# A Fourier transform along the model dimension: from a product of weight and table to a transform of the values, with its own pipeline

## The chip, the cores and the metric

The kernel runs on one core of one Trainium2 chip. The metric is the device time of one execution in microseconds; before the change it is 658.19 us, the median of 3 runs (657.83 to 658.28). Engines are called PE (TensorE; its weight load PEld), DVE (VectorE), ACT (ScalarE), POOL (GpSimd) and SP (SyncE, which only issues transfers here).

## What is computed

```python
bucket = pack(q @ proj > 0), pack(k @ proj > 0)
attn   = softmax(where(bucket_q == bucket_k, q @ k.T / 8, -1e9)) @ v
x      = attn as (2, 768, 512)
gate   = sigmoid(causal 5-tap convolution of x along s with conv_w)
x2     = (gate * (x @ w_val)) @ w_out
u      = x2 + Re(FFT_d(FFT_s(x2)))
un     = (u - mean(u)) / sqrt(var(u) + 1e-6)
out    = u + relu(un @ w_ch1) @ w_ch2
```

There are 2 batches, 768 positions s, 512 channels d, and 2048 hidden units. Weights arrive as 64-bit floats. The kernel works in a 32-bit format of PE with short mantissas; each factor is kept as a high and a low part, and each product is made of three: high x high, high x low, low x high.

## The kernel before

The work goes through three phases, and on each engine the instructions stand in the order in which the program issues them (nothing is reordered by a scheduler).

`attention()` runs over 96 blocks and ends with the products with w_val of batch 0 (tiles `early` and `late`, L199). In its last two turns DVE also computes the convolution of channel chunk 2 of batch 1 (`conv_dve`, L219 to L226), and POOL splits x into high and low parts (`x_split`, L186 to L189).

`mixing()` has the rest of the first MoE block and the two Fourier transforms. Of the transform along d only 258 columns are computed (NL; 257 cosines or sines and one of padding), the other 255 mirror them; that along s is folded: `even_odd` (L925 to L937) makes the sum and the difference of position s and 768 - s of the gated values. DVE makes them in `gt` (L935 for 383 columns, L936 for one), ACT the high part `gh` (L929), POOL the low part `gl` (L930). With s = 0 (sum) and s = 1 (difference) there are two parts per batch, each of 4 chunks of channels (c) and 3 blocks of 128 folded positions (kt). In order:

- w_out is converted to high and low parts chunk by chunk (`from64`, L125 to L157: DVE L139, ACT L142, DVE L145, L146, L149, L150, L157, ACT L162), with the temporaries `cv` in SBUF. Between the chunks stand the products with w_val of batch 1 (`val`) and the gates (L207). POOL computes the convolution of chunk 3 (L215, L217) and the splits `xsl` (L189).
- PE transposes w_out (L974, 32 of them) and multiplies it with the table of cosines and sines: L984, 8 groups of 12 matmuls of 258 columns. ACT and DVE split the results into `wah` and `wal` (L989, L990).
- For each batch: 7 groups of 12 matmuls of 258 columns give the folded values times that product (L1003 in `gmm`, split into `ah` and `al`, L1016 and L1017); then, for each kt, `own` (12 matmuls of 512 columns with w_out for each s; L1003 too), `mixed` (the transform along s of ah and al, L1049, with a copy by ACT, L1051), `total` (DVE adds both, L1056, L1058, L1061), and POOL makes two blocks of u from sum and difference (L1073). For batch 0 `center` follows (DVE L866 to L868: mean, variance, subtraction), and its transposes (L880, with L883 and L884) stand between the groups of batch 1.
- In batch 1, `channel_split(kt)` for kt = 0 and 1 converts the first weights of the MLP (the same steps L139 to L150, and POOL L155) after the sums of kt and ahead of its u additions.

`channel()` is the MLP: `first` (L1109), relu and split (L1111, L1112), `second` (L1121).

The lines that differ on the way to a single product with the table are the two following; everything else is in the functions below.

```python
pa[:, :NL], w[:, c, m * P : (m + 1) * P], wide[:, x, c, part * NL : (part + 1) * NL],
gmm(pa[:, :NL], b, s, m, lambda c: wah[:, c, part, :], lambda c: wal[:, c, part, :])
```

Of the kernel before, what the change touches and what calls it, by code (L numbers as in the profile page):

```python
# [17 lines left out]
P = 128  # L18
# [30 lines left out]
def dft_tables():  # L49

    d = np.arange(DM)
    l = np.arange(NL)
    ang = 2.0 * np.pi * ((d[:, None] * l[None, :]) % DM) / DM
    cs = 2.0 * np.concatenate([np.cos(ang), np.sin(ang)], axis=1)
    ch, cl = split12(cs)
    wide = np.stack([ch, cl], 0).reshape(2, NC, P, 2 * NL).transpose(2, 0, 1, 3)
# [43 lines left out]
def block_kernel(  # L100
# [118 lines left out]
    def conv_dve(c, i):  # L219

        x, dst = xT[1], g[1][:, c, :]
        if i == 0:
            nc.vector.tensor_scalar_mul(dst, x[:, c, 0:S], cwt[:, 0, c : c + 1])
        for kk in (1, 2) if i == 0 else (3, 4):
            nc.vector.scalar_tensor_tensor(
                dst, x[:, c, kk : kk + S], cwt[:, kk, c : c + 1], dst, op0=ALU.mult, op1=ALU.add  # L226
            )


    def attention(es):  # L230
# [488 lines left out]
        for n in range(NT + 2):  # L719
# [82 lines left out]
            if n >= NT:  # L802
                conv_dve(2, n - NT)
# [7 lines left out]
        for c in range(NC):  # L811
            x_split(1, 0, c, nc.vector)
        for c in range(NC):
# [72 lines left out]
    def mixing(es):  # L886
        mp = pool(es, "mp")
        ps = pool(es, "psx", 8, psum=True)

        def psum():  # L890
            return ps.tile([P, 512], F32, tag="ps", name="ps")
# [3 lines left out]
        wah = mp.tile([P, NC, 2, NL], F32R, name="wah")  # L895
        wal = mp.tile([P, NC, 2, NL], F32R, name="wal")


        ep = pool(es, "ep", 2)
        seq = ep.tile([P, 2, 2, 3, HS], F32R, name="seq", bufs=1)  # L900
        odd = ep.tile([P, 2, P], F32R, name="odd", bufs=1)
        vs = ExitStack()
        vp = pool(vs, "vp", side="right")
        conv_tmp = xT[0].rearrange("p c t -> p (c t)")[:, :S]
        gts = [ep.tile([P, HS], F32, name=f"gt{i}", bufs=1) for i in range(4)]
        rs = ExitStack()
        rp = pool(rs, "rp")
        raws = [rp.tile([P, DM], I64, name=f"wor{c}") for c in range(NC)]
        for c in range(NC):
            nc.sync.dma_start(raws[c], w_out[c * P : (c + 1) * P, :])  # L910
        toh = vp.tile([P, NC, DM], F32R, name="toh")
        tol = vp.tile([P, NC, DM], F32R, name="tol")
        wide = vp.tile([P, 2, NC, 2 * NL], F32R, name="wide")
        xsplit[1, 1] = tuple(vp.tile([P, NC, HS], F32R, name=f"xs{i}") for i in "hl")


        gh, gl = {}, {}

        def parts_tiles(b, pl):
            for s in range(2):  # L920
                gh[b, s] = pl.tile([P, NC, HS], F32R, tag=f"gh{s}", name="gh", bufs=1)
                gl[b, s] = pl.tile([P, NC, HS], F32R, tag=f"gl{s}", name="gl", bufs=1)

# [15 lines left out]
        wo = [from64(rp, raws[c], woh[:, c, :], wol[:, c, :], half=True) for c in range(NC)]  # L939
# [6 lines left out]
        nc.gpsimd.dma_start(wide, t_wide)  # L946
        for i in range(6):
            conv_pool(1, 3, i, conv_tmp)
        for c in range(NC):
            x_split(1, 1, c)  # L950
        for c in range(3):
            sigmoid(1, c)
        for i in range(6, 9):
            conv_pool(1, 3, i, conv_tmp)
        nc.gpsimd.dma_start(seq, t_seq)
        nc.gpsimd.dma_start(odd, t_odd)
        for c in range(NC):
            val(0, c)
        for c in range(NC):
            run(wo[c])  # L960
            val(1, c)
            if c == 3:
                sigmoid(1, 3)
                nc.scalar.activation(warm, warm, AF.Sqrt)
            gate(1, 0, c, pvs[0, c])
        for c in range(NC):
            gate(1, 1, c, pvs[1, c])


        for c in range(NC):  # L970
            for i, (w, to) in enumerate(((woh, toh), (wol, tol))):
                pw = psum()
                for m in range(NC):
                    nc.tensor.transpose(pw[:, m * P : (m + 1) * P], f32(w)[:, m, c * P : (c + 1) * P], ident)  # L974
                nc.scalar.copy(to[:, c, :], pw)
        rs.close()
        pp = pool(es, "pp")
        parts_tiles(0, pp)
        for i, (m, part) in enumerate((m, part) for part in range(2) for m in range(NC)):
            pa = psum()  # L980
            n = 0
            for w, x in ((toh, 0), (toh, 1), (tol, 0)):
                for c in range(NC):
                    nc.tensor.matmul(  # L984
                        pa[:, :NL], w[:, c, m * P : (m + 1) * P], wide[:, x, c, part * NL : (part + 1) * NL],
                        start=n == 0, stop=n == 3 * NC - 1,
                    )
                    n += 1
            nc.scalar.copy(wah[:, m, part, :], pa[:, :NL])  # L989
            nc.vector.tensor_tensor(wal[:, m, part, :], pa[:, :NL], f32(wah)[:, m, part, :], op=ALU.subtract)  # L990
# [4 lines left out]
        vs.close()  # L995
        xs.close()
        m2 = pool(es, "m2", 2)

        def gmm(dst, b, s, m, wh, wl):
            n = 0  # L1000
            for x, w in ((gh[b, s], wh), (gh[b, s], wl), (gl[b, s], wh)):
                for c in range(NC):
                    nc.tensor.matmul(  # L1003
                        dst, x[:, c, m * P : (m + 1) * P], w(c), start=n == 0, stop=n == 3 * NC - 1
                    )
                    n += 1

        parts_tiles(1, m2)
        for b in range(B):
            ah = m2.tile([P, 2, 4, NL], F32R, tag="ah", name="ah", bufs=1)  # L1010
            al = m2.tile([P, 2, 4, NL], F32R, tag="al", name="al", bufs=1)
            todo = [(0, m, 0, m) for m in range(3)] + [(1, 0, 0, 3)] + [(1, m, 1, m) for m in range(3)]
            for i, (s, m, part, slot) in enumerate(todo):
                pa = psum()
                gmm(pa[:, :NL], b, s, m, lambda c: wah[:, c, part, :], lambda c: wal[:, c, part, :])
                nc.scalar.copy(ah[:, part, slot, :], pa[:, :NL])  # L1016
                nc.vector.tensor_tensor(al[:, part, slot, :], pa[:, :NL], f32(ah)[:, part, slot, :], op=ALU.subtract)  # L1017
                if b == 0:
                    even_odd((1, i // 4, i % 4))
                    if i == 6:  # L1020
                        even_odd((1, 1, 3))
                        even_odd()
                        gs.close()
                        late_tiles()
                        channel_load(0)
                        channel_load(1)
                elif i < 6:
                    u_transpose(0, i, psum)
            for kt in range(3):
# [172 lines left out]
```

## Time and profile before

| | |
|---|---|
| median of 3 runs | 658.19 us (657.83 to 658.28) |
| profiled execution | 658.59 us, span 656.8 us |
| granted PE clock, mean | 0.995 |
| PE busy | 636.2 us (97%) |
| DVE busy | 454.3 us (69%) |
| ACT busy | 357.6 us (54%) |
| POOL busy | 275.2 us (42%) |

The span reaches from the first to the last instruction; the execution's own time has 1.8 us more around it. Times in the views count from the start of the span. A row of a timeline gives the start of a group of equal instructions, how long the group lasted, the engine, line, operation, output <- inputs and the count; in brackets how long the engine waited before it and for which instruction. A row of the chain gives start, length and what it was, for the chain of work that ended last. The granted clock is a share of 2.4 GHz.

### The profile page before, as it was taken

The numbers are of one execution on the slowest core, as the hardware profiler recorded it, in microseconds if no ns is written. First come the engines' busy times: TensorE is split into PE (matmuls) and PEld (weight loads), VectorE is DVE, ScalarE is ACT, GpSimd is POOL, SyncE is SP. The second block draws the span as 40 slices with busy tenths as digits, with TensorE's granted clock in tenths as the row PEclk, the third lists the DMA queues.
The fourth block names the chain that finished last, engine by engine and source line by source line (L and its number), as shares of the span: only waits on it lengthen the run. The fifth ranks groups of instructions, "written<-read, shape, count | busy, mean of one in ns | idle before, by whom it ended". The sixth has DMA issues, their size and how long they took to land.

```text
span 656.8 us, 10829 instructions
## 1 busy us (share of the span) xinstructions
PE 636.2 (97%) x3954; PEld 597.1 (91%) x3954; DVE 454.3 (69%) x832; ACT 357.6 (54%) x707; POOL 275.2 (42%) x285
## 2 busy tenths in 40 slices
PE   7999999999999999969999989999999999999997
PEld 6899999999999999869989878999999899999996
DVE  4998999999898987987756478899886511111113
ACT  5888989888798996355313345555665211111110
POOL 7132578788788698925531343333332000000000
PEclk9999999999999999979999999999999999999999
DMA  6957465675755303450000123444441100000002
GB/s 157 202 124 169 128 160 126 145 181 132 188 130 132 92 17 114 153 216 1 1 1 1 54 76 129 128 129 129 128 130 64 70 26 1 0 1 1 0 1 96
DMA packets 54061, 61.32 MB, mean 93 GB/s; under 512 B 28936, under 2 KB 42332, under 8 KB 53752
## 3 DMA queue, kind: packets, MB, share of 16 engines
q1 hardware_dynamic: 53272, 56.02, 32.1%
q0 software_dynamic: 432, 4.60, 1.9%
q8 instruction: 31, 0.51, 0.3%
q14 instruction: 22, 0.18, 0.1%
q10 hardware_dynamic: 304, 0.01, 0.0%
HBM read 35.04 MB, written 3.15 MB: 58 GB/s over the span
## 4 chain that ended last, share of the span: by engine, by line
PE 80%; DVE 11%; POOL 3%; issue 2%; ACT 1%; SPq 1%; DMA 1%; DVEq 0%; POOLq 0%; ACTq 0%
PE pf L1109 19%; PE acc L1121 19%; PE sp L469 8%; PE ps L1003 8%; PE op L529 8%; PE ptp L506 7%; PE ps L1049 2%; PE bp L346 2%; DVE ptl L518 1%; DVE sd L481 1%; PE ptp L601 1%; DVE cv L149 1%; DVE cv L146 1%; PE ps L974 1%; POOL g L217 1%
## 5 line engine op out<-in xcount | busy, mean ns | idle before, releaser
L1121 PE MATMUL acc<-w,hid 128*128 128x512 f32 x576 | 137.1, 390 | 0.0
L1121 PEld LDWEIGHTS acc<-w,hid 128*128 128x128 f32 x576 | 107.4, 188 | 19.8
L1112 DVE SCALAR_TENSOR_TENSOR hid<-pf,hid 128x384 fp32r<-128x384 f32 x60 | 32.2, 555 | 120.0 <-ACT hid L1111 120.0
L481 DVE TENSOR_SCALAR_CACHE_REDUCE sd<-sp 128x768 f32<-128x768 f32 x96 | 91.0, 948 | 16.1 <-PE sp L469 15.2
L518 DVE TENSOR_TENSOR ptl<-ptp,pth 128x768 fp32r<-128x768 f32 x96 | 91.4, 952 | 5.9 <-ACT pth L514 5.9
L1109 PE MATMUL pf<-uth,w 128*128 128x384 f32 x480 | 94.7, 338 | 0.2 <-POOL w L155 0.2
L514 ACT CAST pth<-ptp 128x768 fp32r<-128x768 f32 x96 | 77.3, 805 | 31.0 <-PE ptp L506 13.6
L469 PE MATMUL sp<-k,q 128*128 128x384 f32 x384 | 90.8, 358 | 3.0 <-DVE sd L481 1.7
L488 ACT ACTIVATE sd<-sd,nm 128x768 f32<-128x768 f32 x96 | 90.7, 944 | 2.7 <-DVE sd L481 2.7
L1111 ACT ACTIVATE hid<-pf 128x384 fp32r<-128x384 f32 x60 | 28.0, 488 | 113.9 <-PE pf L1109 113.9
L1109 PEld LDWEIGHTS pf<-uth,w 128*128 128x128 f32 x480 | 85.6, 187 | 3.0 <-POOL w L155 0.5
L155 POOL TENSOR_TENSOR w<-cv 128x512 fp32r<-128x512 f32 x32 | 41.4, 1293 | 107.9 <-DVE cv L150 95.5
L506 PE MATMUL ptp<-ident,sd 128*128 128x128 f32 x576 | 78.6, 273 | 0.2 <-ACT sd L488 0.2
L529 PE MATMUL op<-ptl,v 128*128 128x256 f32 x288 | 73.8, 285 | 0.0
L529 PE MATMUL op<-pth,v 128*128 128x256 f32 x288 | 73.8, 283 | 0.0
L469 PEld LDWEIGHTS sp<-k,q 128*128 128x128 f32 x384 | 62.3, 189 | 6.3 <-DVE sd L481 4.1
L506 PEld LDWEIGHTS ptp<-ident,sd 128*128 128x128 f32 x576 | 65.8, 141 | 1.0 <-ACT sd L488 0.5
L547 POOL TENSOR_TENSOR xm<-xc,xs 64x256 f32<-64x256 f32 x48 | 36.1, 751 | 67.8 <-ACT sd L488 31.6
L142 ACT ACTIVATE cv<-cv,col 128x512 int32<-128x512 int32 (+1 forms) x37 | 26.5, 716 | 57.6 <-DVE cv L139 57.6
L529 PEld LDWEIGHTS op<-ptl,v 128*128 128x128 f32 x288 | 54.7, 190 | 0.9 <-issue 0.2
L529 PEld LDWEIGHTS op<-pth,v 128*128 128x128 f32 x288 | 54.6, 190 | 0.0
L1109 PE MATMUL pf<-utl,w 128*128 128x384 f32 x240 | 52.1, 338 | 0.0
(222 smaller groups left out, 1118.2 us busy)
## 6 DMA issues: line engine op xcount, KB each, us to landing
raw<-in_moe_w_ch_dram SPq DMA_DIRECT2D x32, 512.0 KB, 3.7
q<-ht SPq DMA_DIRECT2D x30, 192.0 KB
k<-ht SPq DMA_DIRECT2D x30, 192.0 KB, 3.1
rqk<-in_q_dram SPq DMA_DIRECT2D x16, 192.0 KB, 3.6
rqk<-in_k_dram SPq DMA_DIRECT2D x16, 192.0 KB, 4.5
rv<-in_v_dram SPq DMA_DIRECT2D x8, 384.0 KB, 3.3
out_dram<-o SPq DMA_DIRECT2D x12, 256.0 KB, 2.1
xs<-xc SPq DMA_DIRECT2D x47, 64.0 KB, 1.9
```

What stands on the lines that cost most here:

```text
L155: nc.gpsimd.tensor_tensor(dst_l, fold(g.bitcast(F32)), fold(e.bitcast(F32)), op=ALU.mult)
L469: nc.tensor.matmul(sp[:, a, :HS], q2[i][:, m, qi * P : (qi + 1) * P], k2[i][:, m, a * HS : (a + 1) * HS], start=m == 1, stop=m == 0,)
L481: nc.vector.tensor_scalar(sd[n].rearrange("p (a c) -> p a c", a=2), sp[:, :, :HS], CLAMP, None, op0=ALU.min, op1=ALU.min, accum_out=st[p][ ...
L488: nc.scalar.activation(sd[n], sd[n], AF.Exp, bias=st[p]["nm"][:, i : i + 1], scale=-1.0, accum_out=st[p]["sums"][:, i : i + 1],)
L506: nc.tensor.transpose(tp[:, r // 3, c0 : c0 + P], sd[n][:, r * P : (r + 1) * P], ident)
L514: nc.scalar.copy(p_parts(n)[0], tp)
L518: nc.vector.tensor_tensor(lo, tp, f32(ho), op=ALU.subtract)
L529: nc.tensor.matmul(po[kb], v3[:, r, c0 : c0 + P], pt[kb][x][:, r, :], start=r == 0 and x == 0, stop=r == R - 1 and x == 1,)
L547: add[kb] = lambda: nc.gpsimd.tensor_tensor(st[p]["xm"][mr, blk * QB : (blk + 1) * QB], xc[mr, :], xs[mr, :], op=ALU.add)
L1003: nc.tensor.matmul(dst, x[:, c, m * P : (m + 1) * P], w(c), start=n == 0, stop=n == 3 * NC - 1)
L1109: nc.tensor.matmul(pf[:, :HS], w[:, c, :], x[:, c, cs], start=n == 0, stop=n == 3 * NC - 1)
L1121: nc.tensor.matmul(acc, x[:, ts_], w, start=f == 0 and n == 0, stop=f == NF - 1 and n == 2)
```

## The change

The two-step product (w_out times table, then values times that) is replaced: the values times w_out (`own`), which were computed anyway, are now also the input of the transform along d.

- `fold`: ACT copies the own product to `y` (L1013); DVE adds or subtracts columns d and 512 - d (L1016), which gives 256 columns in place of 512.
- `turn`: PE transposes these (2 blocks of 128, and for the cosine part a third with the column d = 0; L1024, L1026); ACT and DVE split them into high and low parts `ft` (L1031, L1032).
- `along_d`: PE multiplies them with the table `tab` (6 matmuls of 258 columns, and 2 more with `first` for d = 0 in the cosine part; L1043), ACT and DVE split the result into `ah` and `al` (L1046, L1047).
- `mixed` and `total` stay in what they compute; `total` adds from PSUM into `y` (L1069 to L1074), and the u additions are at L1084, all in `both(b, kt)`.
- The pipeline runs over 12 jobs (b, kt, s): turn i issues `own` and `fold` of job i, `along_d` of job i - 2, `turn` of job i - 1. The three `both(0, kt)` all stand in turn 7; the transposes of u of batch 0 in turns 11 to 13; the three `both(1, kt)` behind the pipeline, the first two followed by `channel_split(kt)`, which now stands behind the u additions.
- The transposes of w_out and the product with the table are gone (32 transposes, 8 x 12 matmuls), and so are the 14 groups of 12 with wah and wal. New are 36 transposes and 100 matmuls of 258 columns.
- `out_weights(c)` converts w_out with temporaries in PSUM instead of SBUF (L923 to L938). The pool of 8 PSUM banks becomes one of 6 and one of 2.
- The convolutions of chunks 2 and 3 of batch 1 become `conv_act`: five products on ACT and four additions on POOL. The splits of x for the second half of batch 0 go from POOL to DVE (L772). `even_odd` of batch 1 stands in the first five turns of the pipeline, with two buffers `gt` of each kind cut to one.
- The loads of w_out are issued into a pool of its own; the table is half as large.

```diff
-    def conv_dve(c, i):
+    def conv_act(c):
         x, dst = xT[1], g[1][:, c, :]
+        for kk in range(5):
+            to = dst if kk == 0 else xT[0][:, kk - 1, :S]
+            nc.scalar.activation(to, x[:, c, kk : kk + S], AF.Copy, scale=cwt[:, kk, c : c + 1])
+        for kk in range(1, 5):
+            nc.gpsimd.tensor_tensor(dst, dst, xT[0][:, kk - 1, :S], op=ALU.add)
...
-                    x_split(0, 1, c)
+                    x_split(0, 1, c, nc.vector)
...
+        def out_weights(c):
+            words = raws[c].bitcast(I32).rearrange("p (n two) -> p n two", two=2)
+            lo, hi = words[:, :, 0], words[:, :, 1]
+            a, g_ = (psum(pw).bitcast(I32) for _ in range(2))
+            e = rp.tile([P, DM], I32, tag="cve", name="cv")
+            nc.vector.tensor_scalar(a, hi, 0x7FFFFE00, None, op0=ALU.bitwise_and)
+            nc.scalar.activation(a, a, AF.Relu, scale=8.0, bias=col[:, 4:5])
+            nc.vector.tensor_scalar(g_, hi, 0x1FF, 15, op0=ALU.bitwise_and, op1=ALU.logical_shift_left)
+            nc.vector.scalar_tensor_tensor(g_, lo, 17, g_, op0=ALU.logical_shift_right, op1=ALU.bitwise_or)
+            nc.vector.scalar_tensor_tensor(a, hi, -(2 ** 31), a, op0=ALU.bitwise_and, op1=ALU.bitwise_or)
+            nc.vector.tensor_scalar(e, a, -(2 ** 23), None, op0=ALU.bitwise_and)
+            nc.vector.scalar_tensor_tensor(
+                wol[:, c, :], g_, 2.0 ** -35, e.bitcast(F32), op0=ALU.mult, op1=ALU.mult
+            )
+            nc.scalar.copy(woh[:, c, :], a.bitcast(F32))
...
+        out_weights(0)
+        conv_act(3)
+        for c in range(2):
+            val(1, c)
+        out_weights(1)
+        even_odd((0, 0, 0), (0, 1, 0))
+        sigmoid(1, 2)
+        gate(1, 0, 2, pvs[0, 2])
+        for c in range(2):
+            gate(1, 1, c, pvs[1, c])
+        for c in range(2, NC):
+            val(1, c)
+        even_odd((0, 0, 1), (0, 1, 1))
+        out_weights(2)
+        even_odd((0, 0, 2), (0, 1, 2))
+        out_weights(3)
+        even_odd((0, 0, 3), (0, 1, 3))
+        even_odd()
...
+        def fold(b, s, kt, yp):
+            y = ys[b, s, kt] = m2.tile([P, DM], F32, tag="y", name="y", bufs=8)
+            nc.scalar.copy(y, yp)
+            for part in (s,) if s == 0 or kt else (0, 1):
+                fo = folds[b, s, kt, part] = m2.tile([P, 2 * P], F32, tag="fold", name="fold", bufs=3)
+                nc.vector.tensor_tensor(
+                    fo, yp[:, 1:257], y[:, 511:255:-1], op=ALU.subtract if part else ALU.add
+                )
...
+            fh, fl = turned[b, s, kt, part] = [
+                m2.tile([P, 3, P], F32R, tag=f"f{x}", name="ft", bufs=2)[:, :n] for x in "hl"
+            ]
+            src = pt[:, : n * P].rearrange("p (n t) -> p n t", n=n)
+            nc.scalar.copy(fh, src)
+            nc.vector.tensor_tensor(fl, src, f32(fh), op=ALU.subtract)
...
+        def along_d(b, s, kt, part):
+            fh, fl = turned[b, s, kt, part]
+            ops = [(x[:, i, :], tab[:, part, w, i, :]) for x, w in ((fh, 0), (fh, 1), (fl, 0)) for i in range(2)]
+            if part == 0:
+                ops += [(x[:, 2, :], first) for x in (fh, fl)]
...
+        for i in range(len(jobs) + 2):
+            if i < len(jobs):
+                fold(*jobs[i], own(*jobs[i]))
+            if i > 1:
+                for x in spans(jobs[i - 2]):
...
+                    along_d(*x)
+            if 0 < i <= len(jobs):
+                for x in spans(jobs[i - 1]):
+                    turn(*x)
             if i < 4:
-                even_odd((0, 0, i), (0, 1, i))
+                even_odd((1, 0, i), (1, 1, i))
...
+            elif i == 7:
+                for kt in range(3):
+                    both(0, kt)
+            elif i > 10:
+                for x in range(2):
+                    u_transpose(0, 2 * (i - 11) + x, psum)
+        for kt in range(3):
+            both(1, kt)
+            if kt < 2:
+                channel_split(kt)
```

The order changes at three places. The first is DVE between the products with w_val and the first product of the transform: from the second conversion of w_out on, before.

```order
L139 TENSOR_SCALAR cv<-wor_3860 128x512
L145 TENSOR_SCALAR cv<-wor_3860 128x512
L146 SCALAR_TENSOR_TENSOR cv<-wor_3860,cv 128x512
L149 SCALAR_TENSOR_TENSOR cv<-wor_3860,cv 128x512
L150 TENSOR_SCALAR cv<-cv 128x512
L157 SCALAR_TENSOR_TENSOR wol<-cv 128x512
L207 TENSOR_TENSOR g_74<-ps,g_74 128x384
L139 TENSOR_SCALAR cv<-wor_3861 128x512
```

From the second step of the same conversion on, now (`gt` are the folds of the values over s, `g_74` the gates of batch 1):

```order
L931 TENSOR_SCALAR ps<-wor_3871 128x512
L932 SCALAR_TENSOR_TENSOR ps<-wor_3871,ps 128x512
L933 SCALAR_TENSOR_TENSOR ps<-wor_3871,ps 128x512
L934 TENSOR_SCALAR cv<-ps 128x512
L935 SCALAR_TENSOR_TENSOR wol<-ps,cv 128x512
L952 TENSOR_TENSOR gt_3866<-g_73 128x383
L953 TENSOR_TENSOR gt_3866<-g_73 128x1
L952 TENSOR_TENSOR gt_3867<-g_73 128x383
L953 TENSOR_TENSOR gt_3867<-g_73 128x1
L210 TENSOR_TENSOR g_74<-ps,g_74 128x384 x3
L952 TENSOR_TENSOR gt_3868<-g_73 128x383
```

The folds of batch 0, which stood behind all four conversions and beside the product with the table, now stand between the conversions.

The second is DVE in turn 7, where the three blocks of batch 0 are: the end of the last of them, and what follows, now (`st`, `mu` and `u_4312` are the centering, `fold`, `a` and `ft` the pipeline).

```order
L1069 TENSOR_TENSOR y<-y,ps 128x257
L1074 SCALAR_TENSOR_TENSOR y<-ps,y 128x255
L868 BN_STATS st<-u_4312 128x6
L869 BN_AGGR mu_4313<-st 128x2
L870 TENSOR_SCALAR u_4312<-u_4312,mu_4313 128x512
L868 BN_STATS st<-u_4312 128x6
L869 BN_AGGR mu_4313<-st 128x2
L870 TENSOR_SCALAR u_4312<-u_4312,mu_4313 128x512
L1016 TENSOR_TENSOR fold<-ps,y 128x256
L1047 TENSOR_TENSOR a<-ps,a 128x258
L1032 TENSOR_TENSOR ft<-ps,ft 128x384
L1032 TENSOR_TENSOR ft<-ps,ft 128x256
```

All sums and centerings of batch 0 stand ahead of the low halves `ft` of the job that is turned in turn 8; before, batch 0 was centered block by block between its own products.

The third is POOL at the end of the transform, before:

```order
L1073 TENSOR_TENSOR u_4413<-eo 128x512 x6
L155 TENSOR_TENSOR w_0_4427<-cv 128x512
L1073 TENSOR_TENSOR u_4415<-eo 128x512 x2
L155 TENSOR_TENSOR w_0_4429<-cv 128x512
L1073 TENSOR_TENSOR u_4415<-eo 128x512 x4
```

and now:

```order
L1084 TENSOR_TENSOR u_4312<-y 128x512 x6
L1084 TENSOR_TENSOR u_4314<-y 128x512 x2
L158 TENSOR_TENSOR w_0_4326<-cv 128x512
L1084 TENSOR_TENSOR u_4314<-y 128x512 x2
L158 TENSOR_TENSOR w_0_4328<-cv 128x512
L1084 TENSOR_TENSOR u_4314<-y 128x512 x2
```

The two additions of a block of u of batch 1 are now issued ahead of the step of the MLP weight that shares their place in the program.

## Rows read from the trace of the kernel before

**Rows 1.** page, part 1: busy time and share of each engine

```profile
PE 636.2 (97%) x3954; PEld 597.1 (91%) x3954; DVE 454.3 (69%) x832; ACT 357.6 (54%) x707; POOL 275.2 (42%) x285
```

**Rows 2.** windows, 397 to 647 us: busy time of each engine, granted clock

```profile
397.00:647.00 250.00, 249.94 (x1272) 228.23 (x1271) 122.08 (x226) 88.42 (x160) 34.93 (x27) 1.00 0.19 60
```

**Rows 3.** timeline, PE, 377.5 to 397: start, us, instructions, [wait <-what ended it]

```profile
380.29 1.56 PE L1109 MATMUL acc<-uth,w 128*128 128x384 f32 x8
...
386.13 0.97 PE L1109 MATMUL acc<-uth,w 128*128 128x384 f32 x4 [1.49 <-ACT w L162]
...
391.06 4.29 PE L1121 MATMUL acc<-w,hid 128*128 128x512 f32 x18
...
396.28 0.96 PE L1109 MATMUL pf<-uth,w 128*128 128x384 f32 x4 [0.23 <-POOL w L155]
```

**Rows 4.** timeline, PE, 254 to 310

```profile
286.51 0.33 PE L974 MATMUL ps<-ident,woh 128*128 128x128 f32 x1 [2.31 <-ACT woh L162]
290.17 0.48 PE L974 MATMUL ps<-ident,woh 128*128 128x128 f32 x1 [3.32 <-ACT woh L162]
...
308.21 0.39 PE L1003 MATMUL ps<-wah,gh 128*128 128x258 f32 x1 [0.41 <-ACT gh L929]
```

**Rows 5.** windows of 0.5 us: busy time of each engine, then PEclk

```profile
288.00:288.50 0.50, 0.00 (x0) 0.00 (x0) 0.47 (x2) 0.50 (x1) 0.00 (x0) 0.50 1.24 508
...
295.00:295.50 0.50, 0.50 (x8) 0.50 (x6) 0.00 (x0) 0.50 (x2) 0.00 (x0) 1.00 0.00 0
```

**Rows 6.** chain of waits, 300 to 400 us: start, us, what

```profile
324.25 5.58 PE ps L1003 x24
...
346.35 0.44 PE ps L880 x4
346.79 1.45 PE ps L1003 x12
```

**Rows 7.** timeline, DVE, 262 to 301

```profile
274.45 0.77 DVE L139 TENSOR_SCALAR cv<-wor 128x512 int32<-128x512 int32 x1
...
281.14 2.20 DVE L157 SCALAR_TENSOR_TENSOR wol<-cv 128x512 fp32r<-128x512 int32 x1
...
283.73 0.41 DVE L139 TENSOR_SCALAR cv<-wor 128x512 int32<-128x512 int32 x1
...
286.30 0.69 DVE L157 SCALAR_TENSOR_TENSOR wol<-cv 128x512 fp32r<-128x512 int32 x1
```

**Rows 8.** timelines of PE, POOL and ACT, 262 to 300

```profile
268.68 0.85 PE L199 MATMUL ps<-xl,wvh 128*128 128x384 f32 x4
...
277.19 2.31 POOL L217 TENSOR_TENSOR g<-g,xT 128x768 f32<-128x768 f32 x1
...
290.02 0.84 ACT L192 ACTIVATE g<-g 128x768 f32<-128x768 f32 x1
```

**Rows 9.** groups of DVE, 60 to 240 us (the attention): busy, mean ns

```profile
L696 DVE SCALAR_TENSOR_TENSOR cvp<-wvr,cvp 128x256 int32<-128x256 int32 x7 | 2.9, 419 | 0.0
```

**Rows 10.** chain of waits, 256 to 310 us

```profile
298.74 0.07 DVE gt L936
...
301.51 0.89 DVE gt L936
```

**Rows 11.** page, part 6: issues of DMA, KB each, us to landing

```profile
raw<-in_moe_w_ch_dram SPq DMA_DIRECT2D x32, 512.0 KB, 3.7
```

**Rows 12.** timeline, DVE, 324 to 333

```profile
327.16 0.43 DVE L1056 TENSOR_TENSOR eo<-ps,mix 128x257 f32<-128x257 f32 x1 [3.07 <-PE ps L1003]
327.50 0.47 DVE L1061 SCALAR_TENSOR_TENSOR eo<-mix,col,ps 128x255 f32<-128x255 f32 x1
...
331.74 0.49 DVE L868 TENSOR_SCALAR u<-u,mu 128x512 f32<-128x512 f32 x1
```

**Rows 13.** timeline, DVE, 377.5 to 397

```profile
381.23 0.42 DVE L139 TENSOR_SCALAR cv<-raw 128x512 int32<-128x512 int32 x1
...
385.46 0.43 DVE L150 TENSOR_SCALAR cv<-cv 128x512 int32<-128x512 int32 x1
```

More of the change, by code (lines that the diff above doesn't have):

```diff
@@ L970, in mixing @@
[L970 to L980, printed above, removed]
+        out_weights(1)
@@ new lines, in mixing @@
+        even_odd((0, 0, 0), (0, 1, 0))
+        sigmoid(1, 2)
+        gate(1, 0, 2, pvs[0, 2])
+        for c in range(2):
+            gate(1, 1, c, pvs[1, c])
+        for c in range(2, NC):
[6 more added lines that the diff above has]
+        even_odd()
+        sigmoid(1, 3)
+        nc.scalar.activation(warm, warm, AF.Sqrt)
+        gate(1, 1, 2, pvs[1, 2])
@@ L981, in mixing, with own @@
+        for a in range(2):
+            gate(1, a, 3, pvs[a, 3])
+        def own(b, s, kt):
+            yp = psum()
             n = 0
-            for w, x in ((toh, 0), (toh, 1), (tol, 0)):
+            for x, w in ((gh[b, s], woh), (gh[b, s], wol), (gl[b, s], woh)):
                 for c in range(NC):
                     nc.tensor.matmul(
-                        pa[:, :NL], w[:, c, m * P : (m + 1) * P], wide[:, x, c, part * NL : (part + 1) * NL],
-                        start=n == 0, stop=n == 3 * NC - 1,
+                        yp, x[:, c, kt * P : (kt + 1) * P], w[:, c, :], start=n == 0, stop=n == 3 * NC - 1
@@ new lines, in mixing @@
+        sums = {}
+        def along_d(b, s, kt, part):
[3 more added lines that the diff above has]
+                ops += [(x[:, 2, :], first) for x in (fh, fl)]
+            pa = psum()
+            for n, (x, w) in enumerate(ops):
+                nc.tensor.matmul(pa[:, :NL], x, w, start=n == 0, stop=n == len(ops) - 1)
+            ah, al = sums[b]
+            slot = kt if part == s else 3
+            nc.scalar.copy(ah[:, part, slot, :], pa[:, :NL])
+            nc.vector.tensor_tensor(al[:, part, slot, :], pa[:, :NL], f32(ah)[:, part, slot, :], op=ALU.subtract)
@@ new lines, in mixed @@
+        def mixed(b, s, kt):
+            ah, al = sums[b]
+            ks = slice(kt * P, (kt + 1) * P)
+            ops = []
+            for x, w in ((ah, 0), (ah, 1), (al, 0)):
+                for jt in range(3):
+                    ops.append((seq[:, s, w, jt, ks], x[:, s, jt, :]))
+            if s == 0:
+                ops += [(odd[:, 0, :], ah[:, 0, 3, :]), (odd[:, 0, :], al[:, 0, 3, :])]
+            elif kt == 0:
+                for jt in range(3):
+                    ops += [(odd[:, 1, :], ah[:, 0, jt, :]), (odd[:, 1, :], al[:, 0, jt, :])]
+            pm = psum()
+            for n, (w, x) in enumerate(ops):
+                nc.tensor.matmul(pm[:, :NL], w, x, start=n == 0, stop=n == len(ops) - 1)
+            return pm
@@ new lines, in both @@
+        def both(b, kt):
+            pm = [mixed(b, s, kt) for s in range(2)]
+            for s in range(2):
+                total(b, s, kt, pm[s])
+            for t, op in ((kt, ALU.add), (3 + kt, ALU.subtract)):
+                nc.gpsimd.tensor_tensor(u[b][:, t, :], ys[b, 0, kt], ys[b, 1, kt], op=op)
+                if b == 0:
+                    center(b, t)
+        rs.close()
+        vs.close()
+        xs.close()
+        m2 = pool(es, "m2")
+        gts = [m2.tile([P, HS], F32, name=f"gt{i}") for i in range(2)] * 2
```

184 lines of the change are left out of this document (60 added, 124 removed).

## The prediction, before the kernel was run

> **What bounds the kernel now.** I read the page first: TensorE (PE) is busy 97% of the span [rows 1]. So the span is PE's work plus the places where PE waits, and these are found from PE's timeline and the chain of waits. The reader should look in each for the column at the end that names what ended a wait. From 397 us on PE is busy 249.94 of 250 us [rows 2]; whatever this change does ends before, and moves the end by as much as it moves the wait for the third channel weight at 396.28 us [rows 3]. I count up to that mark.
>
> Between the products with w_val and that mark there are three stages. (a) 284 to 308 us: PE waits twice for converted rows of w_out, 2.31 and 3.32 us, then transposes them, multiplies them with the table, and starts on the values at 308.2 after a wait of 0.41 us [rows 4]. The granted clock falls to 0.50 in this gap (1.2 of 2.4 GHz) and is back at 1.00 only 4.8 us after PE resumes at 290.17 [rows 4, 5]. (b) 308.2 to 380.3 us: PE runs without a gap; the chain holds PE alone [rows 6]. (c) 380.3 to 396.3 us: the MLP's first weights come late, with waits of 1.49 us at first and 0.23 us at the mark [rows 3].
>
> What makes stage (a) long is VectorE (DVE): the last step of a conversion takes 0.69 us alone, and 2.20 us beside GpSimd (POOL) additions [rows 7].
>
> **PE's work.** Prices are the spacing of matmuls in stage (b): 1.45 us for 12 of 258 columns, 0.121 each; 5.58 for 24 of 512, 0.233 each; 0.44 for 4 transposes, 0.11 each [rows 6]. Removed: 32 transposes and 96 matmuls of the table product, all ahead of 308.2, and 14 groups x 12 = 168 matmuls in stage (b), 168 x 0.121 = 20.3 us. Added in stage (b): 36 transposes, 4.0 us, and 100 matmuls of 258 columns, 12.1 us. The 12 own products and the 132 mixed ones (132 x 0.121 = 15.9) stay. Stage (b) so loses 4.2 us of PE work, and the work ahead of it goes. If nothing on another engine were late, the gain would be some 11 us: the first product could start at about 301 rather than 308.2 and 4.2 us come off behind it. I walked the new order to see what is late.
>
> **The start (a).** The first product now needs all four chunks of w_out and all four folded chunks of the values (the order on DVE: conversion 0, conversion 1, fold 0, gates, fold 1, conversion 2, fold 2, conversion 3, fold 3). DVE is free at about 269.9, when the second product with w_val has ended [rows 8]. Terms:
> - Four conversions. An old one took 8.8 us beside POOL (274.45 to 283.3) and 3.2 us alone (283.73 to 286.95) [rows 7]. The new ones keep their temporaries in PSUM. In the attention part such a step took 419 ns for 256 columns in the mean, with POOL at work beside it, and at 512 columns I estimate 0.60: six steps and 0.35 for the gaps between them are 3.95 us [rows 9]. Bounds are 3.2 and 8.8; I take 3.95, since the row with PSUM operands is the nearest: 15.8 us in all.
> - ScalarE (ACT) gets five 128x768 convolution products (a sigmoid of that shape takes 0.84 [rows 8]; I take 0.74, 3.7 us) between the first and the second conversion; the second waits for its rescaling on ACT: 2.35 us.
> - Four folds with two operands in SBUF. Each is an operation of 383 columns, 0.47 us, and one of a single column, 0.07 us alone and 0.89 beside POOL [rows 10], so a pair is 1.08 us alone and 2.7 held twice. The first stands beside POOL additions of 2.31 us [rows 8]: I take 3.4. Then 2.05 (POOL free for a half), 3.0, and for the last only the half that the product waits for with its copy on ACT, 2.05: 10.5 us. Bounds are 4.3 (none held) and 12.
> - Three gates of 0.5: 1.5 us.
>
> 269.9 + 15.8 + 2.35 + 10.5 + 1.5 = 300.05 us, **8.15 us earlier** than 308.2. PE has then waited some 18 us and starts at half clock, as before at 290.17: at 4.8 us of half speed I charge 2.2 us, less 0.7 for matmuls that can start on the first three chunks: +1.5. The loads of w_out are moved behind the last products of batch 0, on the queue of SP, to about 264.6; a load of this size lands in 3.7 us [rows 11], so the first is there at 268.3, before DVE reaches it at 269.9, and the later ones have 4 us each; were they late, the start would move by as much. The table of half the size stands on POOL's queue ahead of its splits and is first read by the products along d, some 8 us behind the start: nothing.
>
> **The stream (b).** -4.2 us of work, +1.5 of clock. Then one wait. All three blocks of batch 0 (mixed products, sums, additions, centering) are issued in one place, at i = 7. PE is through 66 mixed products in 7.9 us and has two own products, 6 matmuls along d, and one set of transposes left: 7.6 us, so it reaches the next matmuls along d at 15.5. These need the low half of the transposed fold, which DVE computes behind all three blocks. Per block DVE has four sums, each begun 0.34 us behind the one before (327.16, 327.50), 1.4 us in all, and the second centering ends 4.17 us after the last sum, since both wait for POOL's additions of the sums (327.97 to 332.15) [rows 12]. From the first sum's end at 3.95: 3.95 + 4.17 + 2 x 5.55 = 19.2, then fold, correction and two low halves: 20.35. PE waits 20.35 - 15.5 = **4.85 us**, where it waited for nothing. Behind it DVE catches up, since each of its steps (about 0.4 us, four a job) is shorter than a job of PE. Stage (b): -4.2 + 1.5 + 4.85 = **+2.2 us**.
>
> **The tail (c).** The own products of batch 1 now lie ahead of its mixed products, so at the end PE has 7.9 us of these and nothing to cover DVE's sums and the splits of the first MLP weights. Moved past each other are POOL's u additions, now ahead of the splits. From the first mixed product: first sums end at 3.95; split 0 then runs beside two POOL additions, as the split at 381.23 did, 4.6 us [rows 13]: 8.55; sums 9.95; split 1, 4.75: 14.7; sums 16.1. Only then are the banks free for the MLP's first product. PE has waited 8.2 us; it needs 4.2 us at full clock and 2.2 more at a fallen one: 22.5. The second half takes 4.2 (24 matmuls of 384 columns, 12 in 2.1 us from 380.29 [rows 3]): 26.7; then 4.8 of the 5.2 that lie between 391.06 and the mark [rows 3], since the weight is then there: 31.5. Before, 16.0 us lay between PE's last DFT product and the mark; now 31.5 - 7.9 = 23.6: **+7.6 us**.
>
> Sum: -8.15 + 2.2 + 7.6 = +1.6 us on the profiled execution's 658.59, 660.2; that execution lies 0.4 above the median of the runs shown, so 659.8 against 658.19. The change saves PE work and gives it back as waits for DVE.
>
> **Rivals.**
> - The clock falls in the new wait of the stream (chance 0.16). For: the gap at 284 did it (0.50 at 288.0 us, two waits of 2.31 and 3.32 us with one transpose between them [rows 4, 5]). Against: behind the wait of 1.49 us at 386, four products of 384 columns still took 0.97 us and 18 of 512 columns 4.29, as at full clock [rows 3]; 4.85 us lies between these two cases. Price as at the start, 2.2 us: 662.0. By a rule of the Trainium skill ("TensorE: Matmul & The Clock Gate", Part 1: The HAM clock gate) the half rate is the idle state and the window free-running, so the same wait may or may not cost it; by that, 662.0 about as often as 659.8. The row with 0.50 agrees as to the idle state.
> - Faster (0.30): the preparation on DVE runs unhindered. If conversions take 3.2 us, and the folds 1.08 a pair from the second on, the start comes at 292 to 296; it decides below 297. For: a one-column operation took 0.07 us once and 0.89 another time with the same neighbours [rows 10], so how much is blocked depends on what POOL does just then. Against: POOL has its subtractions in that stretch. At 296: 660.2 - 4.05 - 0.4 = 655.7; at 292.5, 652.
> - The conversions are blocked as the old ones were (0.14): 8.8 us for each of the first two. Part of this lies beside the waits that I count for ACT and the first fold: that fold would end at 269.9 + 17.6 + 1.1 = 288.6 instead of 283.55, so +5.05: 664.9. For: old rows [rows 7]; against: [rows 9]. The Trainium skill ("SBUF — State Buffer", Who interferes with whom) says that DVE with at most one input from SBUF doesn't contend with GpSimd outside its two-port modes; by it this case falls away, and 659.8 stands. The trace agrees as far as the 419 ns go.
> - The change pays in full (in the 0.30 too, as its far end): 647 if DVE were never late. The order on DVE speaks against it, since sums stand ahead of what PE needs.
>
> **Chances.** My forecast 0.40 (657 to 662), clock 0.16, unhindered 0.30, blocked 0.14. A measurement tells about 0.2% from no change, 1.3 us: faster is below 656.9, slower above 659.5. Faster 0.30, from the unhindered case; same 0.18, the lower half of my own; slower 0.52. Range 653 to 665.5: from most of the unhindered case to the blocked one.
>
> **What would show it.** The first own product at about 300, with half clock at its start; DVE conversion steps near 0.60 us beside POOL; one PE wait of 4 to 5 us some 48 us later, released by DVE's low half; about 8 us of PE wait at the end of the DFT, released by DVE's last sum, with splits of 4.6 us beside POOL's additions; from there on PE without gaps. It is wrong if PE's stream has no gap, if the start comes before 297 or after 304, or if the MLP's first product starts less than 5 us after the last mixed one.

## The result: 661.83 us against 658.24, and the profile after

The changed kernel takes 661.83 us (median of 4 runs, 660.97 to 663.04), the kernel before 658.24 us (4 runs): a ratio of 1.0057, interval 1.0039 to 1.0074. That is slower, as forecast, by 3.6 us where 1.6 was forecast, and inside the range. Beside the experiments the kernel before ran 48 more times: two of these took 2223.64 and 3575.51 us and are left out, the other 46 lie between 657.0 and 661.9, and one of them is above the lowest of the changed kernel's four. The profiled execution took 661.77 us (span 660.0), 3.2 us more between first and last instruction than before.

The page of the changed kernel, parts 1 and 2 (busy time; granted clock in tenths over 40 slices of the span), beside [rows 1]:

```profile
PE 621.7 (94%) x3794; PEld 581.4 (88%) x3794; DVE 454.0 (69%) x851; ACT 365.4 (55%) x715; POOL 268.4 (41%) x282
...
PEclk9999999999999999968997979999999999999999
```

PE is busy 14.5 us less, in a longer span: the work that was saved came back as waiting. The balance up to the mark that the forecast counts to, the wait for the third channel weight, shows it best. The windows from 262 us to the mark, before and after (length, then PE's busy time):

```profile
262.00:396.28 134.28, 124.73 (x782) 115.13 (x780) 95.23 (x172) 50.56 (x103) 60.71 (x50) 0.97 0.19 64
```

```profile
262.00:399.48 137.48, 109.16 (x619) 98.56 (x617) 97.63 (x188) 56.38 (x108) 60.00 (x50) 0.89 0.19 65
```

PE is busy 15.6 us less there and idle 28.3 us instead of 9.6, 18.8 more: together 3.2 us longer, although the half clock is inside its busy time. Three dips of the clock (slices 18 and 19, 22, and 24) show where. PE's timeline of the changed kernel names the waits:

```profile
284.01 0.47 PE L1003 MATMUL ps<-woh,gh 128*128 128x512 f32 x1 [2.15 <-ACT gh L946]
291.23 0.79 PE L1003 MATMUL ps<-woh,gh 128*128 128x512 f32 x1 [6.75 <-ACT gh L946]
297.88 1.62 PE L1003 MATMUL ps<-woh,gh 128*128 128x512 f32 x2 [5.86 <-ACT gh L946]
...
330.49 1.34 PE L1063 MATMUL ps<-a,seq 128*128 128x258 f32 x9
...
351.36 0.80 PE L1043 MATMUL ps<-tab,ft 128*128 128x258 f32 x2 [5.10 <-DVE ft L1032]
...
367.95 1.33 PE L1063 MATMUL ps<-a,seq 128*128 128x258 f32 x9
...
383.99 2.90 PE L1162 MATMUL acc<-uth,w 128*128 128x384 f32 x8 [7.89 <-DVE y L1074]
...
399.48 0.96 PE L1162 MATMUL pf<-uth,w 128*128 128x384 f32 x4 [0.26 <-POOL w L158]
```

Two single products, for the first two chunks of channels, go ahead at 284.01 and 291.23. The stream of own products starts at 297.88, 10.3 us ahead of the 308.21 of [rows 4]. Then PE waits 5.10 us for the low half of a transposed fold, and 7.89 us for DVE's last sum, between the end of the transform and the MLP. The mark, the 396.28 of [rows 3], is now 399.48: 3.2 us later, as much as the span is longer.

### The profile page after: what moved, and what is told of

Its sections match the earlier page's. It is cut to its first block, busy times and chain, and to the rows that moved or that the text cites. A ratio compares the mean times of both kernels' runs of the same rounds, so it can differ in the third digit from the quotient of the medians.

```text
span 660.0 us, 10541 instructions
## 1 busy us (share of the span) xinstructions
PE 621.7 (94%) x3794; PEld 581.4 (88%) x3794; DVE 454.0 (69%) x851; ACT 365.4 (55%) x715; POOL 268.4 (41%) x282
## 4 chain that ended last, share of the span: by engine, by line
PE 83%; DVE 11%; ACT 2%; issue 1%; POOL 1%; DMA 1%; SPq 0%; DVEq 0%; POOLq 0%
PE pf L1162 19%; PE acc L1174 19%; PE sp L471 9%; PE op L531 9%; PE ptp L508 8%; PE ps L1003 5%; PE bp L348 2%; PE ps L1043 2%; PE acc L1162 2%; PE early L202 1%; DVE sd L483 1%; PE late L202 1%; PE ptp L603 1%; DVE ptl L520 1%; PE ps L1063 1%
## 5 line engine op out<-in xcount | busy, mean ns | idle before, releaser
L145 ACT ACTIVATE cv<-cv,col 128x512 int32<-128x512 int32 (+1 forms) x33 | 23.6, 715 | 44.5 <-DVE cv L142 44.5
```

## The experiments

Times below are medians with their range; the kernel before, run beside each group, had medians of 658.3 to 658.4. "Less" and "more" are against the changed kernel's 661.83. Differences of about 1 us are within the spread of the runs.

**The wait in the middle.** DVE of the changed kernel, the end of the centerings and what PE waits for:

```profile
349.69 0.48 DVE L870 TENSOR_SCALAR u<-u,mu 128x512 f32<-128x512 f32 x1
350.09 0.42 DVE L1016 TENSOR_TENSOR fold<-ps,y 128x256 f32<-128x256 f32 x1
350.42 0.42 DVE L1047 TENSOR_TENSOR a<-ps,a 128x258 fp32r<-128x258 f32 x1
350.75 0.88 DVE L1032 TENSOR_TENSOR ft<-ps,ft 128x384 fp32r<-128x384 f32 x2
```

```diff
-                if b == 0:
-                    center(b, t)
...
+            elif i in (8, 9, 10):
+                center(0, i - 8)
+                center(0, i - 5)
```

> One edit: the six centerings of batch 0 are issued on VectorE in turns 8, 9 and 10 of the pipeline, two in each, instead of in turn 7 ahead of the low half that TensorE waits for. My theory (that low half is late because sums and centerings of all three blocks stand before it): TensorE's wait of 5.10 us at 351.36 goes (under 0.5 us left), and with it the stretch at half clock from 351 to 357 us, 2.8 us more; 7.9 us in all, 661.8 becomes about 654. Rival (VectorE has too much work in the pipeline in any order, so that the wait only moves to the next turns): waits of 3 to 5 us in sum between 350 and 370 us, under 3 us gained.

Measured 655.45 us (654.73 to 655.83), 6.4 less. The wait is gone. The same low halves on DVE:

```profile
343.37 0.42 DVE L1016 TENSOR_TENSOR fold<-ps,y 128x256 f32<-128x256 f32 x1 [2.71 <-ACT y L1013]
344.13 0.43 DVE L1047 TENSOR_TENSOR a<-ps,a 128x258 fp32r<-128x258 f32 x1 [0.34 <-ACT a L1046]
344.54 0.89 DVE L1032 TENSOR_TENSOR ft<-ps,ft 128x384 fp32r<-128x384 f32 x2
```

They come 6.2 us earlier, and DVE even waits 2.71 us ahead of them: it was not too much work, but its order. The stretch between the first mixed products of the two batches shrinks from 37.46 us (330.49 to 367.95) to 29.52, 7.9 as expected:

```profile
331.70 1.34 PE L1063 MATMUL ps<-a,seq 128*128 128x258 f32 x9
...
361.22 1.32 PE L1063 MATMUL ps<-a,seq 128*128 128x258 f32 x9
```

Some 0.8 us of the gap to 6.4 is at the end, where half clock lasted 5.5 us past the end of the 7.89 us wait, instead of 3.8 in the changed kernel. The rest is ahead of the edit: in this profile the first mixed block comes 1.2 us later (331.70), with nothing changed before it.

**The clock in that wait.** Products that keep PE busy, without moving anything else:

```diff
             pa = psum()
+            if (b, s, kt) == (1, 1, 0) and part == 0:
+                for _ in range(28):
+                    nc.tensor.matmul(pa[:, :HS], woh[:, 0, 0:P], woh[:, 1, 0:HS], start=True, stop=True)
```

> Against the changed kernel 28 products of 384 columns, overwritten by the next one in the same bank, fill TensorE's wait in the middle (346 to 351 us). They measure the fallen clock there by itself. My theory (half clock from 351 to 357 us costs 2.8 us): the granted clock stays at 1.00, the wait for VectorE's low half ends at the same time, 2.8 us gained: 659.0. Rival (VectorE, still behind after the wait, would hold TensorE at full clock too): a new wait of 1 to 3 us in the next two turns, and 661 to 662.

Measured 659.68 us (658.97 to 660.8), 2.15 less. The windows around the wait (busy time of each engine, then the granted clock), changed kernel and then this one:

```profile
350.00:352.00 2.00, 0.64 (x3) 0.64 (x4) 1.97 (x6) 0.00 (x0) 0.00 (x0) 0.56 0.00 0
352.00:354.00 2.00, 2.00 (x11) 2.00 (x11) 0.43 (x1) 0.46 (x2) 0.00 (x0) 0.50 0.00 0
...
356.00:358.00 2.00, 2.00 (x8) 1.61 (x7) 0.00 (x0) 0.00 (x0) 0.00 (x0) 0.73 0.00 0
```

```profile
350.00:352.00 2.00, 1.72 (x12) 1.51 (x10) 1.96 (x6) 0.00 (x0) 0.00 (x0) 1.00 0.00 0
352.00:354.00 2.00, 2.00 (x15) 1.92 (x16) 1.12 (x4) 0.97 (x3) 0.00 (x0) 1.00 0.00 0
```

The clock holds at 2.4 GHz, PE gets through 15 instructions from 352 to 354 us instead of 11, and the stretch between the two mixed blocks falls from 37.46 to 34.94 us (330.99 to 365.93 here): the fallen clock is worth 2.5 us in the changed kernel's profile. The expected 2.8 counted its whole length; 0.28 us came back as a wait for the same low half. The price isn't fixed: in the five other profiles in which the middle has the same wait and no other of a microsecond (e3, e6, e7, e8, e10) the stretch took 36.1 to 37.3 us, 1.2 to 2.3 above 34.94.

**The tail.** In the changed kernel DVE converts the second MLP weight, then makes the last sums:

```profile
378.30 1.48 DVE L148 TENSOR_SCALAR cv<-raw 128x512 int32<-128x512 int32 x1
379.82 1.63 DVE L149 SCALAR_TENSOR_TENSOR cv<-raw,cv 128x512 int32<-128x512 int32 x1
...
383.42 0.41 DVE L1074 SCALAR_TENSOR_TENSOR y<-ps,y 128x255 f32<-128x255 f32 x1
```

First try, conversions in turns 10 and 11:

```diff
+            if i in (10, 11):
+                channel_split(i - 10)
         for kt in range(3):
             both(1, kt)
-            if kt < 2:
-                channel_split(kt)
```

> One edit: the conversions of the first two MLP weights are issued in turns 10 and 11 of the pipeline instead of behind the sums of blocks 0 and 1 of batch 1. My theory (the MLP's first product waits for VectorE's last sum, which stands behind these two conversions of 4.6 us): the wait of 7.89 us at 383.99 shrinks to about 1, the clock stays at its full rate there (2.2 us more), and 1 to 2 us come back as a wait for the third conversion as in the kernel before: about 7.5 us, 661.8 becomes 654.3. Rival (the additions of u on GpSimd or the sums themselves set that wait): it stays over 5 us and under 3 us are gained.

Measured 659.44 us (658.51 to 661.01), 2.4 less: the rival's gain, but not for its reason. The wait at the end did shrink, from 7.89 to 0.94 us, but a new one stood in the middle:

```profile
369.89 1.03 PE L1043 MATMUL ps<-tab,ft 128*128 128x258 f32 x6 [2.56 <-ACT ft L1031]
...
382.20 1.62 PE L1162 MATMUL acc<-uth,w 128*128 128x384 f32 x8 [0.94 <-DVE y L1074]
```

ACT of the same run shows why: its part of the second conversion waits for DVE and stands ahead of the high half that PE needs.

```profile
367.06 0.72 ACT L145 ACTIVATE cv<-cv,col 128x512 int32<-128x512 int32 x1 [1.26 <-DVE cv L142]
368.12 0.63 ACT L157 ACTIVATE cv<-cv 128x512 f32<-128x512 int32 x1 [0.34 <-DVE cv L149]
368.67 0.62 ACT L165 CAST w<-cv 128x512 fp32r<-128x512 f32 x1
369.19 0.37 ACT L1046 CAST a<-ps 128x258 fp32r<-128x258 f32 x1
369.46 0.38 ACT L1031 CAST ft<-ps 128x256 fp32r<-128x256 f32 x1
```

Behind this wait the clock fell too. The windows show that it did so 1.1 us after PE was at work again, and that it came back 3.4 us later:

```profile
370.50:371.00 0.50, 0.50 (x7) 0.50 (x6) 0.50 (x2) 0.35 (x2) 0.04 (x1) 1.00 0.95 377
371.00:371.50 0.50, 0.50 (x5) 0.50 (x4) 0.50 (x2) 0.33 (x1) 0.00 (x0) 0.53 0.49 197
```

In turns 11 and 12 PE has little work per turn, so nothing covers a late step. The same conversions in turns 5 and 6 (the line reads `if i in (5, 6): channel_split(i - 5)`):

> Against the changed kernel only the conversions of the first two MLP weights move, to turns 5 and 6, far from the transposed folds that e2_splits_early delayed; the centerings stay in turn 7. My theory (the tail's wait is those two conversions ahead of the last sums, and e2 lost its gain to the place): the wait of 7.89 us becomes 0.9, waits of 0.9 in all come behind it, no half clock at the end, nothing new in the pipeline: 8 us gained, 653.8. Rival (a conversion costs the same wherever it stands, because VectorE is full): under 4 us gained, as in e2_splits_early, 658 or more.

Measured 654.42 us (653.67 to 654.71), 7.4 less. PE, at the end:

```profile
376.89 1.64 PE L1162 MATMUL acc<-uth,w 128*128 128x384 f32 x8 [0.94 <-DVE y L1074]
381.93 0.96 PE L1162 MATMUL acc<-uth,w 128*128 128x384 f32 x4 [0.61 <-ACT w L165]
383.15 0.97 PE L1162 MATMUL acc<-uth,w 128*128 128x384 f32 x4 [0.25 <-POOL w L158]
```

So the tail's wait is the order of conversions and sums, and where they stand decides what moving them is worth: 7.4 us in turns in which PE has work, 2.4 in turns in which it has little. In the profile the stretch from the first mixed product of batch 1 to the mark is 7.3 us shorter (367.78 to 392.01).

**Middle and tail together**, centerings in turns 9 to 11, conversions in turns 6 and 8:

> The centerings of batch 0 as in e1_center_later but in turns 9, 10 and 11, and the conversions of the first two MLP weights in turns 6 and 8, further ahead than in e2_splits_early, where their steps stood on ScalarE and VectorE ahead of the last transposed folds and TensorE waited 2.56 us for those. My theory (waits of the middle and of the tail are two separate costs of the order on VectorE; the new wait of e2 came from the place only): no wait over 1 us between 305 and 380 us, the MLP's first product less than 1.5 us behind the last mixed one, no half clock there; against e1_center_later 7.0 us of wait and 3 us of clock go and 0.9 of small waits come: about 646.5. Rival (VectorE and ScalarE are full in the pipeline wherever conversions stand): a wait of 2 to 3 us and a fallen clock in the middle, about 651 to 653.

Measured 649.47 us (649.12 to 649.75), 12.4 less and 0.9866 of the kernel before (0.9847 to 0.9885). Nearly additive (6.4 + 7.4 = 13.8, though in other turns than in those two runs); 1.62 us of wait for a low half stayed at 361.76, since the last centerings stood one turn too late: with them in turns 8 to 10, in e9 below, there is none.

**The start.** Three tries on the 30 us between DVE's first conversion and the first product. The convolution of chunk 3 behind the second conversion (`conv_act(3)` moved below `out_weights(1)`):

> One edit: the convolution of channel chunk 3 of batch 1 (five products on ScalarE, four additions on GpSimd) is issued behind the second conversion of w_out instead of ahead of it. My theory (the start is set by VectorE's chain, in which the second conversion waits 2.67 us for ScalarE): that wait goes and the first own product comes up to 2.7 us earlier; the four additions move by about the same on GpSimd and hold more of the folds, so I take 1 to 2 us, 660.3. Rival (the start hangs on GpSimd's additions, whose end is what lets the folds go): no gain, or a later start, 661.8 to 663.

Measured 665.18 us (664.86 to 665.71), 3.4 more: the rival's sign, and more than it gave. The first pair of folds ended at 278.9 instead of 283.4, but then the sigmoid of chunk 2 stood behind the products on ACT, and GpSimd's additions, now from 279.4 to 287.1, held the second pair:

```profile
282.59 1.49 DVE L210 TENSOR_TENSOR g<-ps,g 128x384 f32<-128x384 f32 x3 [3.73 <-ACT g L195]
284.00 1.49 DVE L952 TENSOR_TENSOR gt<-g 128x383 f32<-128x383 f32 x1
285.41 1.75 DVE L953 TENSOR_TENSOR gt<-g 128x1 f32<-128x1 f32 x1
...
287.55 2.64 DVE L953 TENSOR_TENSOR gt<-g 128x1 f32<-128x1 f32 x1
```

The pair takes 6.1 us instead of 2.1. An addition cost DVE something wherever a fold met it. The edits of e1, e2 and e3 together:

> The edits of the three other runs together. My theory (three separate waits, each with its own cause, so that gains add up): 7.9 + 7.5 + 1.5 = 16.9 us less, 645, and below the kernel before by about 13. Rival (behind these waits stands another bound, such as VectorE's load in the pipeline or the MLP weights): 650 to 656, about as fast as the kernel before.

Measured 658.24 us (655.79 to 659.05): 2 us above the rival's range. Two of the three edits hadn't done what was expected, and those of e1 and e2 get in each other's way: beside the centerings PE waits 2.78 and 1.22 us for high halves from ACT, so that 2.0 us of the middle's 7.9 remain (35.48), while the tail keeps its gain (24.18 us from the first mixed product of batch 1 to the mark, for 31.53). Next, conversions first and folds after the additions, with the convolution's products in the gaps of ACT:

```diff
+        out_weights(0, lambda: conv_act(3, (0, 1)))
...
+        out_weights(1, lambda: conv_act(3, (2, 3)))
...
+        out_weights(2, lambda: (conv_act(3, (4,)), sigmoid(1, 2)))
...
         out_weights(3)
...
+        for c in range(NC):
+            even_odd((0, 0, c), (0, 1, c))
```

> Only the order between the products with w_val and the first own product is changed: the four conversions of w_out stand one behind the other on VectorE, with the convolution products of chunk 3 on ScalarE between the steps of each, and the folds over s come behind them, when GpSimd's four additions are over. My theory (VectorE's chain is the start; it contains 2.67 us of waiting for ScalarE and several us in which the folds are held by GpSimd, while conversions with PSUM temporaries are not held): conversions end at about 285.5, the start is at about 291 instead of 297.9, 7 us gained: 655. Rival (e3_conv_later showed that additions moved later hold other folds: the holding only moves to GpSimd's subtractions of the folds themselves): the start at 295 or later, under 3 us gained.

Measured 657.89 us (657.0 to 658.76), 3.9 less. Conversions ended at 285.6 as expected, but the last chunk of the first product came at 294.45, not 291: the additions were over, and the subtractions of the low parts on GpSimd held four of the one-column operations of the folds (0.95 us instead of 0.15), three of them ahead of that chunk. Both theories had half of it.

```profile
292.90 0.94 DVE L955 TENSOR_TENSOR gt<-g 128x1 f32<-128x1 f32 x1
...
294.45 0.80 PE L1002 MATMUL ps<-woh,gh 128*128 128x512 f32 x1 [1.88 <-ACT gh L948]
```

One part undone, the conversion's temporaries back in SBUF:

> One part of the change undone: the two integer temporaries of the conversion of w_out lie in SBUF again instead of PSUM; order and steps stay. My theory (steps with two operands in SBUF are held by GpSimd, steps with one in PSUM are not): the first two conversions take 7 to 9 us instead of 4.0 (without the wait for ScalarE), and the start comes 4 to 6 us later: 666 to 668. Rival (the place of the temporaries does nothing): conversions take 3.2 us, since a step in SBUF is shorter when alone, and the time is 660 to 662.

Measured 664.29 us (664.01 to 665.04), 2.5 more, between the two. The fourth DVE step of the second conversion, in the changed kernel and then here (where the end of that conversion is shown as well):

```profile
278.03 0.70 DVE L933 SCALAR_TENSOR_TENSOR ps<-wor,ps 128x512 int32<-128x512 int32 x1 [2.67 <-ACT ps L930]
```

```profile
281.29 2.34 DVE L933 SCALAR_TENSOR_TENSOR cv<-wor,cv 128x512 int32<-128x512 int32 x1
...
286.22 0.55 DVE L952 TENSOR_TENSOR gt<-g 128x383 f32<-128x383 f32 x1
```

In SBUF the first two take 6.0 and 10.3 us (269.90 to 275.90 to 286.22), the last two 3.2; in PSUM each takes 4.0 (the second, the wait for ACT apart, 4.1), beside GpSimd or not. The mechanism is the theory's; the time is less, because the long second conversion outlasts the additions and so spares the first folds. The Trainium skill ("SBUF — State Buffer", Who interferes with whom) says that DVE with at most one input from SBUF doesn't contend with GpSimd outside its two-port modes; the rows with temporaries in PSUM agree (0.70 us beside GpSimd). In SBUF steps with one input were held as well (L931: 2.08 us in the second conversion, 0.41 in the third), which fits only if they ran in such a mode; no run shows that.

The clock at the start:

> 86 products of 384 columns whose results are overwritten are added on TensorE between the products with w_val, to fill most of its wait of 282 to 298 us; everything else is as in the changed kernel. They measure what the fallen clock at the start costs by itself. My theory: the granted clock stays at 1.00 through 298 us, the first own products run at full rate, and with 5.5 us of work at half speed no longer there 2.5 to 2.8 us are gained: 659.2. Rival (the clock there costs nothing, because VectorE is what the first turns wait for): no gain, 661 to 662.

Measured 660.89 us (660.39 to 661.45), 0.9 less, between the two numbers, and the ranges overlap (the changed kernel's begins at 660.97). The clock stays at 1.00 from 296 to 300 us, but the first products then wait 0.80 and 0.33 us for high parts and 0.40 for a low one: at half speed PE was hardly faster than its inputs came. So the clock itself explains at most about 1 us of what the start costs.

**All of it**: the order of e6 with the four sums of `even_odd` ahead of the four differences, 43 filling products, conversions in turns 5 and 6, centerings in turns 8 to 10.

> A version that is to beat both kernels: the start order of e6 with the four folds of the sum ahead of the four of the difference, 43 products on TensorE that fill its wait (results overwritten), the first two MLP weights converted in turns 5 and 6, and the centerings of batch 0 in turns 8, 9 and 10. My theory (the waits of start, middle and tail are separate): the start comes at about 290 and at full clock, and against e5_splits_spread 8 us of start, 2 of clock and 2 of wait in the middle go: about 637 to 640. Rival (with the start moved up, the first turns wait for GpSimd's low parts and for the gates of chunk 3): a start at 290 but waits of several us before 310, 643 to 646.

Measured 639.98 us (639.61 to 640.35): 0.971 of the kernel before (0.9677 to 0.9743), 21.9 us below the changed kernel. PE in the start:

```profile
290.33 1.18 PE L1006 MATMUL ps<-woh,gh 128*128 128x512 f32 x4 [0.52 <-ACT gh L948]
...
294.61 0.50 PE L1006 MATMUL ps<-woh,gh 128*128 128x512 f32 x1 [0.77 <-ACT gh L948]
295.95 0.50 PE L1006 MATMUL ps<-woh,gh 128*128 128x512 f32 x1 [0.85 <-ACT gh L948]
...
299.15 0.44 PE L1027 MATMUL ps<-ident,fold 128*128 128x128 f32 x2 [0.83 <-DVE fold L1019]
```

The mean granted clock is 0.999, and there is no wait over 1 us behind 290 us. With this order the changed kernel is well ahead of the kernel before in its own order. No run gives the kernel before the same care; by an estimate from its rows, without the 9.6 us in which PE idles ahead of its mark and the 2.2 us charged to its half clock it would take some 646 us, still above 640.

## Why the prediction was right, and what it missed

- **Sign and cause: right.** PE's saving turned into waits for what DVE delivers, at three places. Each was named with its place, and the runs that shorten or remove them one by one gain 3.9 (the start, of which a part stays), 6.4 and 7.4 us.
- **The start: forecast 1.7 us too late.** The first mixed block came at 330.49 where the terms gave 332.2. A conversion in PSUM took 3.99 us (forecast 3.95; the steps take 0.69 us and not 0.60, but begin 0.60 to 0.73 us apart), the wait for ACT 2.67 (2.35), the first pair of folds 3.2 (3.4), the gates 1.4 (1.5). DVE was free 0.5 us earlier, and the last half with its copy took about 1.3 instead of 2.05.
- **The stream: the step that failed is the clock.** "One wait" of 4.85 us was 5.10. But the likeliest case left the clock at full rate there, with a chance of 0.16 for the rival in which it falls. It fell, not in the changed kernel alone but in all seven profiles that have this wait (4.97 to 5.10 us), and e11 puts 2.5 us on it in the changed kernel's profile (2.2 forecast). The gap at 284 us was the nearer row than the wait of 1.49 us, and should have had the larger chance. With it in the sum the forecast would have been 662.0. That this meets 661.83 so closely is partly luck: the start was 1.7 us earlier than the terms, and the stream another 1.0 us longer.
- **The tail: right to 0.1 us, in part by luck.** From the first mixed product of batch 1 to the mark the terms gave 31.5; the trace has 399.48 - 367.95 = 31.53. Conversions took 4.6 and PE's wait 7.89 (8.2). But two misses cancel: the first 24 matmuls at the fallen clock took 6.0 us (6.4), and the last piece up to the mark 5.2 (4.8), since the wait for the third weight, which the forecast took away, stayed (0.26). In other runs with this tail unchanged the same stretch took 31.0 to 32.4 us.
- Start 1.7 early and stream 3.2 late move the mark by 1.5 of the 2.0 us by which the median was missed; the rest is within the spread of the runs.
- **The rival with blocked conversions** was rightly low: e7 shows what blocking looks like, and the changed kernel's rows of 0.69 us show none. **Unhindered preparation** didn't come about either; additions and subtractions did hold the folds.
- **"If nothing were late, some 11 us" was wrong.** It took the first product's earliest time as 301. PE is done with w_val at 282, so the bound is much further off; e9 stands 18 us below the kernel before.

## What to carry to other kernels

Work taken off the busiest engine is worth only what the others can deliver earlier: write down, for each engine's queue, what now stands ahead of the step that the busy engine needs next. Steps that nobody waits for soon (centerings, weights for later) belong in turns in which the busy engine has long work, and behind the step that it needs; the same move gained 7.4 us in one turn and 2.4 in another. Count the clock's fall with a wait of the matmul engine of some 5 us, and reckon with it from shorter ones: behind 2.56 us (e2) and 2.78 us (e4) it fell as well, behind 1.62 us (e5) it didn't.

## What the runs showed of the hardware that was not expected

- After waits of nearly the same length the half clock lasted differently long: 5.10 us of wait and a clock below full until 357 us, 5.7 us of work, in the changed kernel; 4.97 us of wait and 3.0 us of it in e10_splits_first:

```profile
352.00:354.00 2.00, 1.58 (x7) 1.58 (x8) 1.03 (x3) 0.31 (x1) 0.00 (x0) 0.50 0.00 0
354.00:356.00 2.00, 2.00 (x11) 1.91 (x10) 0.85 (x2) 0.83 (x3) 0.00 (x0) 0.64 0.00 0
356.00:358.00 2.00, 2.00 (x11) 1.58 (x10) 0.56 (x1) 0.09 (x1) 0.00 (x0) 1.00 0.00 0
```

  Some kernels with such waits spread over 2 us from run to run (660.97 to 663.04 for the changed one) and e9, without them, over 0.7 (639.61 to 640.35). But e3 and e7, with the same waits, spread over 0.9 and 1.0 us in four runs each, so it isn't shown that the clock makes the spread.
- A conversion step in PSUM costs the same 0.69 us beside GpSimd and alone, where one in SBUF with a single input takes 0.41 alone (L929 in the changed kernel and in e7). PSUM was the slower place here, and the one in which GpSimd didn't hold the step up; beside GpSimd the step in SBUF took 1.22 us (e7, second conversion).
